# Turns of the probabilities placed after the odd step's second layer, earlier divisors, and reordered weight sums in a fused attention and feed-forward kernel

## The chip, the cores and the metric

The kernel runs on one core of a Trainium2 chip. The time is the device time of one execution in microseconds (us). The core has five engines with instruction queues of their own that run in order: TensorE (PE, matmuls; its weight loads are listed as PEld), VectorE (DVE), ScalarE (ACT), GpSimd (POOL) and SyncE (SP, which issues all DMAs here). They wait for each other through semaphores.

## What is computed

Attention with a window of 16 and summaries of blocks of 32, and a feed-forward layer on its output. Shapes: 4 batches, 8 heads, 768 positions, 64 numbers a head; d_model 512, d_ff 2048.

```python
k_sum = k.reshape(B, H, nb, block, D).max(axis=3)
v_sum = v.reshape(B, H, nb, block, D).mean(axis=3)
scores_l = scale * np.matmul(q, k.transpose(0, 1, 3, 2))      # kept where |i - j| < 16
scores_s = scale * np.einsum('bhsd,bhnd->bhsn', q, k_sum) + np.log(block)
a = softmax(concatenate([scores_l_m, scores_s]))              # sum + 1e-9 as divisor
attn = np.matmul(a, concatenate([v, v_sum], axis=2))
x = attn.transpose(0, 2, 1, 3).reshape(B * S, H * D)
h = x @ w_in
g = h * np.tanh(softplus(h))
return g @ w_out
```

## The kernel before

**Units, groups, steps.** The 3072 tokens are 12 chunks of 256; two chunks are a group, so there are 6 groups of 512 tokens. A unit is one chunk and one pair of heads: 48 units, numbered 0 to 47, 8 to a group. The feed-forward work of a group is 16 steps, one for each 128 columns of d_ff: 96 steps. Each number is kept as an upper and a lower part, and each product is three matmuls (upper by upper, upper by lower, lower by upper).

**A step** has a first layer (`ff_in`, L502, or `ff_in_pair`, L733), Mish on ACT (`ff_act`, L509), a split of the result into upper `ah` (L518) and lower `al` (L520), and a second layer (`ff_out`, L530, 12 matmuls) that is issued two steps later, so that it finds its split made. Groups 0 and 1 use the plain first layer of 12 matmuls. From step 32 on (groups 2 to 5) two steps are done together as a 2 by 2 block product with seven products instead of eight: `ff_in_pair`, 42 matmuls of 256 columns in four PSUM banks, whose results DVE (L743 to L751) and ACT (L739, L742) combine. It needs seven sums of blocks of the weights for every pair of steps, each in two parts, and seven sums of blocks of x.

**Weight sums.** For each of the eight pairs of steps p of a group the sums are made once, in two halves: `first_sums` (L700, L701, then a rounding on ACT, L691, and a subtraction, L692) and `second_sums` (L706, L707 and two more roundings). Both work in one area of SBUF and store their results with DMAs into a DRAM tile `kept[p]`; two blocks are stored as they are (`keep_blocks`). In steps 19 to 32 each step makes one half, pairs 0 to 6 in turn, and steps 35 and 36 make pair 7. `load_sums` (L718) brings the sums of a pair (7 x 2 parts x 128 KB, 1.83 MB) back into one of two buffers, two pairs ahead, in two DMAs: the first four blocks, then the other three. All DMAs are issued by SP in the order of the program, and a store whose sums are not yet made holds up what is behind it.

**Attention in the pairs.** Two units go through together, every four steps from step 29 on (`begins`: 19, 22, 25, 29, 33, ...). At the odd step i: the scores (`att_scores`, L346) and maxima with the mask added (DVE, L367), the exponents of the first unit on ACT (L378), those of the second inside the next pair. `norms` makes the divisors on DVE (L393, L394) and has POOL multiply the probabilities by them (L398): the first unit at step i, the second at step i + 1. At step i + 2, `turns` transposes both units on PE (L404) and ACT copies them out (L408). At step i + 4 `values` multiplies them by the values (L430), and `x_sum` makes the sums of blocks of x, which wait in a list (`waiting`) and are taken from it by the steps. `loads` issues the queries and keys of a unit two ahead (L304, L322, L323), has POOL copy its key maxima in (L309), and, for the first of a batch's chunks, loads keys (L235) for the maxima (DVE, L273) and values (L239) for the means (DVE, L294) through one buffer in turn.

**The order of a pair** of steps i, i + 1 is written out by hand. PE's queue: first layer, second layer of step i - 2, values and scores (every other pair), turns (in the pairs between), second layer of step i - 1. DVE's: the combining of the products, split of step i, divisors of the second unit, sums of blocks of x, weight sums, maxima, split of step i + 1, divisors of the first unit.

Of the kernel before, what the change touches and what calls it, by code (L numbers as in the profile page):

```python
# [9 lines left out]
F32 = mybir.dt.float32  # L10
# [10 lines left out]
P = 128  # L21
# [4 lines left out]
CH = 256  # L26
# [5 lines left out]
NFC = DFF // P  # L32
# [19 lines left out]
WP = 512  # L52
# [14 lines left out]
def fused_kernel(ctx: ExitStack, tc: tile.TileContext, q0, qk, kt, v0, vw, vs, w_in, w_out, out):  # L67
# [398 lines left out]
    def att_blocks(ps, c, hp, n):  # L466
        g, half = divmod(c, CG)
        if not raws:
            raws.append(stage_words("x_blocks").rearrange("p (b t) -> p b t", b=4))
        k = slice(hp % 2, hp % 2 + n)  # L470
        nc.scalar.copy(x_block(hp // 2, half)[:, k], ps[:, :n * CH].rearrange("p (k q) -> p k q", q=CH))
        made = {(0, 0): (2,), (1, 0): (4,), (0, 1): (6,), (1, 1): (5, 1, 3, 7)}[hp // 2, half]
        return [lambda m=m: x_sum(g, m, k) for m in made]
# [37 lines left out]

    def ff_split(g, fc):

        a = st[g, fc]
        ah = ff.tile([P, TG], F32R, tag="ah", name=f"ah{g}_{fc}")
        al = ff.tile([P, TG], F32R, tag="al", name=f"al{g}_{fc}")

        (nc.scalar.copy if g == 0 else nc.vector.tensor_copy)(ah, a)  # L518
        st[g, fc] = ah, al
        return lambda: nc.vector.tensor_sub(al, a, ah.bitcast(F32))  # L520
# [145 lines left out]
    dram = ctx.enter_context(tc.tile_pool(name="dram", bufs=1, space=bass.MemoryType.DRAM))  # L666
    kept = [dram.tile([P, 7, 2, CH], F32, name=f"w_sums_{p}") for p in range(NFC // 2)]
    whole_steps = WHOLE * NFC
# [12 lines left out]

    def keep(p, part, first, step, t):
        n = t.shape[1] // CH
        nc.sync.dma_start(kept[p][:, first:first + (n - 1) * step + 1:step, part, :], quarters(t).bitcast(F32))

    def keep_blocks(p):
        for part, t in enumerate(home(p)):
            keep(p, part, 0, 1, t[:, CH:3 * CH])

    def split_sums(p, first, step, whole, upper):  # L690
        nc.scalar.copy(upper.bitcast(F32R), whole)  # L691
        nc.vector.tensor_sub(whole.bitcast(F32R), whole, upper)  # L692
        keep(p, 0, first, step, upper)
        keep(p, 1, first, step, whole)

    def first_sums(p):

        hi, lo = home(p)
        w, t = area[:, :2 * WP], area[:, 2 * WP:3 * WP]
        nc.vector.tensor_add(w, hi.bitcast(F32), lo.bitcast(F32))  # L700
        nc.vector.tensor_add(quarters(t), quarters(w)[:, 0::2], quarters(w)[:, 1::2])  # L701
        split_sums(p, 3, 3, t, area[:, 3 * WP:])

    def second_sums(p):
        w, t = area[:, :2 * WP], area[:, 2 * WP:3 * WP]
        nc.vector.tensor_sub(t, w[:, :WP], w[:, WP:])  # L706
        nc.vector.tensor_add(w[:, WP:3 * CH], w[:, WP:3 * CH], w[:, CH:WP])  # L707
        split_sums(p, 4, 1, t, area[:, 3 * WP:])
        split_sums(p, 2, 1, w[:, WP:3 * CH], w[:, :CH])

    def buffer(pair):
        at = pair % 2 * BUFFER
        return grounds["w_early"][:, at:at + BUFFER].rearrange("p (m part f) -> p m part f", m=7, part=2)

    def load_sums(pair):
        if pair < (NG - WHOLE) * NFC // 2:
            for some in (slice(0, 4), slice(4, 7)):
                nc.sync.dma_start(buffer(pair)[:, some].bitcast(F32), kept[pair % (NFC // 2)][:, some])  # L718

    def ff_in_pair(g, fc, pair, between):  # L720
# [4 lines left out]
        def products(*found):  # L725
            ps = ps_w.tile([P, TG], F32, tag="w", name=f"ph{g}_{fc}_{len(banks)}")
            banks.append(ps)
            for half, m in enumerate(found):
                wh, wl = (w[:, (4, 3, 1, 2, 6, 7, 5).index(m), part, :] for part in range(2))
                xh, xl = x_piece(g, m)  # L730
                for a in range(2):
                    for n, (w_, x) in enumerate(((wh, xh), (wh, xl), (wl, xh))):
                        nc.tensor.matmul(turned(ps[:, half * CH:(half + 1) * CH]), w_[:, a * P:(a + 1) * P],  # L733
                                         turned(x[:, a, :]), start=(a == 0 and n == 0), stop=(a == 1 and n == 2))
# [70 lines left out]
    def scores(i):  # L805
# [5 lines left out]
        return some  # L811

    def weight_sums(i):
        p, second = divmod(i - done - 2 * (i > whole_steps), 2)
        if p < NFC // 2 and (i <= whole_steps or i > whole_steps + 2):
            if not second:
                keep_blocks(p)
            (second_sums if second else first_sums)(p)

    for i in range(done, whole_steps):  # L820
        ff_in(*steps[i])
        ff_act(*steps[i])
        values(i)
        for unit_ in scores(i):
            att_exponents(*unit_)
        ff_split(*steps[i])()
        norms(i)
        loads(i)
        for sums_ in waiting[:2]:
            waiting.pop(0)()  # L830
# [7 lines left out]
    for i in range(whole_steps, len(steps), 2):  # L838
        pair = (i - whole_steps) // 2
        ff_in_pair(*steps[i], pair, lambda: [att_exponents(*late_exponents.pop()) for _ in late_exponents[:]])  # L840
        ff_act(*steps[i])
        ff_act(*steps[i + 1])
        ff_split(*steps[i])()
        norms(i)
        while waiting:
# [7 lines left out]
        if some:  # L853
            att_exponents(*some[0])
            late_exponents.extend(some[1:])
        turns(i + 1)
        ff_split(*steps[i + 1])()
        norms(i + 1)
        loads(i + 1)
        for _ in waiting[:2]:  # L860
            waiting.pop(0)()
        ff_out(*steps[i - 1])
        weight_sums(i + 1)
    for i in range(2):
# [45 lines left out]
```

## Time and profile before

| | us |
|---|---|
| median of 3 runs | 680.04 |
| lowest and highest of them | 678.96, 682.68 |
| the profiled execution | 682.73 |
| span of its instructions | 681.0 |
| busy: PE, weight loads, DVE, ACT, POOL | 623.0, 535.1, 465.7, 309.8, 81.5 |
| mean granted clock of TensorE in it | 0.964 of full |

All rows below are of the profiled execution, in us from the start of its span. A matmul's duration is modelled, so a run of matmuls is read by its length as a whole; the waits and the start times are what counts.

### The profile page before, as it was taken

The page shows a single profiled execution, that of the slowest core. Times are in us where ns is not written, and L with a number is a line of the kernel's source. Part 1 is how long each engine was busy: PE and PEld are TensorE (multiplying, and loading weights), DVE is VectorE, ACT ScalarE, POOL GpSimd, SP SyncE. Part 2 cuts the span into 40 slices and gives each one's busy share as a digit, 9 for nine tenths or more (in the row PEclk, how much of TensorE's full clock was granted, in tenths as well). Part 3 has the DMA queues.
Part 4 walks back from the last instruction along what each step waited for, and adds up shares of the span by engine and source line. Part 5 has one row for each costly group of instructions (what it writes and reads, how often), then busy time and mean ns, then how long its engine had stood idle before and what let it go on. Part 6 is the DMA issues. An engine that isn't in the chain of part 4 may idle for free.

```text
span 681.0 us, 12911 instructions
## 1 busy us (share of the span) xinstructions
PE 623.0 (91%) x4848; PEld 535.1 (79%) x4848; DVE 465.7 (68%) x1158; ACT 309.8 (45%) x747; POOL 81.5 (12%) x119
## 2 busy tenths in 40 slices
PE   4799999999999977798988988889889899999997
PEld 3688777788887756687977887779778787998996
DVE  4799999964677688865648567657674474755443
ACT  4786769663555242643525335335263352122121
POOL 4431121110221010101001000010010000000000
PEclk9999999999998997888989999989899898999999
DMA  8787676623567689878547387585494454374421
GB/s 256 214 279 258 217 232 217 209 84 127 186 183 234 203 268 307 273 260 321 169 170 274 132 287 245 198 305 169 164 339 157 152 186 161 119 275 177 153 104 63
DMA packets 56366, 141.77 MB, mean 208 GB/s; under 512 B 8816, under 2 KB 28016, under 8 KB 52208
## 3 DMA queue, kind: packets, MB, share of 16 engines
q1 hardware_dynamic: 56304, 140.94, 61.4%
q8 instruction: 39, 0.64, 0.4%
q14 instruction: 23, 0.19, 0.1%
HBM read 117.83 MB, written 20.97 MB: 204 GB/s over the span
## 4 chain that ended last, share of the span: by engine, by line
PE 39%; DVE 14%; DMA 8%; ACT 4%; POOL 2%; issue 1%; SPq 1%; POOLq 0%; ACTq 0%; DVEq 0%
PE po L530 20%; PE ph L733 14%; DMA w_sums<-results 4%; DMA qk<-qk 3%; DVE al L520 2%; ACT pr L378 2%; POOL pr L398 1%; DVE pr L367 1%; PE x_ps L430 1%; PE pt_ps L404 1%; PE sc L346 1%; DVE ah L518 1%; DMA ks<-kt 1%; DMA vsum<-vs 1%; ACT h L509 1%
## 5 line engine op out<-in xcount | busy, mean ns | idle before, releaser
L530 PE MATMUL po<-w_early_out_hi,ah 128*128 128x512 f32 x240 | 100.5, 419 | 0.0
L733 PE MATMUL ph<-xh,w_early_in 128*128 128x256 f32 x512 | 98.7, 278 | 0.0
L530 PE MATMUL po<-w_early_out_hi,al 128*128 128x512 f32 x240 | 97.8, 408 | 0.9 <-DVE al L520 0.9
L530 PE MATMUL po<-w_early_out_lo,ah 128*128 128x512 f32 x240 | 97.8, 407 | 0.0
L398 POOL TENSOR_TENSOR pr<-pr,rs 128x480 f32<-128x480 f32 x48 | 59.6, 1243 | 292.8 <-DVE rs L394 253.8
L743 DVE TENSOR_TENSOR change<-h,ph 128x256 f32<-128x256 f32 x32 | 13.5, 421 | 102.6 <-ACT h L742 102.5
L733 PEld LDWEIGHTS ph<-xh,w_early_in 128*128 128x128 f32 x512 | 82.7, 189 | 0.0
L378 ACT ACTIVATE pr<-pr,nm 128x120 f32<-128x120 f32 x192 | 73.4, 386 | 12.2 <-DVE nm L367 11.9
L509 ACT ACTIVATE h<-h 128x512 f32<-128x512 f32 x64 | 36.9, 624 | 75.0 <-DVE h L750 75.0
L733 PE MATMUL ph<-xl,w_early_in 128*128 128x256 f32 x256 | 71.0, 277 | 0.0
L739 ACT COPY h<-ph 128x512 f32<-128x512 f32 x32 | 18.8, 587 | 101.6 <-PE ph L733 101.6
L404 PE MATMUL pt_ps<-ident,pr 128*120 128x128 f32 x192 | 32.4, 302 | 29.7 <-POOL pr L398 29.7
L530 PE MATMUL po<-w_late_out_hi,ah 128*128 128x512 f32 x144 | 59.2, 411 | 0.0
L530 PE MATMUL po<-w_late_out_hi,al 128*128 128x512 f32 x144 | 57.5, 399 | 0.0
L530 PE MATMUL po<-w_late_out_lo,ah 128*128 128x512 f32 x144 | 57.4, 399 | 0.0
L530 PEld LDWEIGHTS po<-w_early_out_hi,al 128*128 128x128 f32 x240 | 48.2, 201 | 10.8 <-DVE al L520 2.1
L530 PEld LDWEIGHTS po<-w_early_out_hi,ah 128*128 128x128 f32 x240 | 48.4, 202 | 10.2 <-issue 1.3
L530 PEld LDWEIGHTS po<-w_early_out_lo,ah 128*128 128x128 f32 x240 | 47.7, 199 | 10.4
L404 PEld LDWEIGHTS pt_ps<-ident,pr 128*120 128x120 f32 x192 | 23.2, 146 | 36.6 <-POOL pr L398 33.0
L502 PE MATMUL ph<-xh,w_early_in 128*128 128x512 f32 x160 | 52.0, 391 | 0.0
L520 DVE TENSOR_TENSOR al<-h,ah 128x512 fp32r<-128x512 f32 x64 | 48.4, 756 | 2.2
L733 PEld LDWEIGHTS ph<-xl,w_early_in 128*128 128x128 f32 x256 | 48.6, 190 | 0.0
(111 smaller groups left out, 1251.5 us busy)
## 6 DMA issues: line engine op xcount, KB each, us to landing
w_early_in<-w_sums SPq DMA_DIRECT2D x32, 1024.0 KB
w_early_in<-w_sums SPq DMA_DIRECT2D x32, 768.0 KB
qk<-qk SPq DMA_DIRECT2D x40, 496.0 KB
w<-w_in SPq DMA_DIRECT2D x16, 512.0 KB
w<-w_out SPq DMA_DIRECT2D x16, 512.0 KB
w_sums<-results SPq DMA_DIRECT2D x32, 256.0 KB
vw<-vw SPq DMA_DIRECT2D x40, 192.0 KB
ks<-kt SPq DMA_DIRECT2D x16, 384.0 KB
```

Of the source, the lines that this page charges most:

```text
L346: nc.tensor.matmul(ps[h][row, at0:at0 + KA], u["qk"][r, s, h * QT:(h + 1) * QT], u["qk"][r, s, P:], start=True, stop=True)
L367: nc.vector.tensor_tensor_reduce(out=pr[:, j, :], in0=ps[h][:, at + pair * KA:at + (pair + 1) * KA], in1=m, scale=-SCALE, scalar=-NEG, op0 ...
L378: nc.scalar.activation(pr[:, s, :], pr[:, s, :], AF.Exp, scale=-1.0, bias=nm[:, s:s + 1], accum_out=sm[:, s:s + 1])
L398: nc.gpsimd.tensor_mul(u["p"], u["p"], u["r"].unsqueeze(2).broadcast_to([P, NQ, KA]))
L404: nc.tensor.transpose(ps[:KA, s * P:(s + 1) * P], u["p"][:, s, :], ident)
L502: nc.tensor.matmul(turned(ph), w[:, cc * P:(cc + 1) * P], turned(x[:, cc, :]), start=(cc == 0 and n == 0), stop=(cc == NCC - 1 and n == 2))
L509: nc.scalar.activation(a, st[g, fc], AF.Mish)
L520: return lambda: nc.vector.tensor_sub(al, a, ah.bitcast(F32))
L530: nc.tensor.matmul(turned(po[g][t]), a[:, tok], turned(w), start=(fc == 0 and n == 0), stop=(fc == NFC - 1 and n == 2))
L733: nc.tensor.matmul(turned(ps[:, half * CH:(half + 1) * CH]), w_[:, a * P:(a + 1) * P], turned(x[:, a, :]), start=(a == 0 and n == 0), stop ...
L739: nc.scalar.copy(second, products(1, 3))
L743: nc.vector.tensor_sub(change, second[:, high], ps[:, low])
```

## The change

1. **Turns.** In a pair, `turns(i + 1)` is called after `ff_out(steps[i - 1])` instead of ahead of the split of step i + 1. Since the second layer is PE's and the split is DVE's, this moves the eight transposes of a turn behind 12 matmuls on PE, and their two ACT copies with them.
2. **Divisors.** In a pair, `norms(i)` stands ahead of `ff_split(steps[i])` instead of behind it.
3. **Weight sums.** The halves are made in the order of pairs 5, 0, 1, 2, 3, 4 in steps 19 to 30, none in steps 31 to 35, and pairs 6 and 7 in steps 36 to 39 (`order_of_sums`).
4. **Layout.** `kept[p]` holds the parts ahead of the blocks, and the blocks in an order in which two made together lie side by side, so that a store writes them as one run of 2 KB to a partition instead of two of 1 KB. `load_sums` brings the upper part and then the lower part, seven blocks each.
5. **Steps 19 to 31.** In a step without scores the upper part of the split is made by ACT instead of DVE, and only one waiting sum of x is taken, not two; in a step with scores the upper part is issued ahead of the exponents.
6. **x sums.** The last four of a group are made in the order 1, 5, 3, 7 instead of 5, 1, 3, 7.

```diff
-        made = {(0, 0): (2,), (1, 0): (4,), (0, 1): (6,), (1, 1): (5, 1, 3, 7)}[hp // 2, half]
+        made = {(0, 0): (2,), (1, 0): (4,), (0, 1): (6,), (1, 1): (1, 5, 3, 7)}[hp // 2, half]
...
-    def ff_split(g, fc):
+    def ff_split(g, fc, by_scalar=False):
...
-        (nc.scalar.copy if g == 0 else nc.vector.tensor_copy)(ah, a)
+        (nc.scalar.copy if g == 0 or by_scalar else nc.vector.tensor_copy)(ah, a)
...
-    kept = [dram.tile([P, 7, 2, CH], F32, name=f"w_sums_{p}") for p in range(NFC // 2)]
+    kept = [dram.tile([P, 2, 7, CH], F32, name=f"w_sums_{p}") for p in range(NFC // 2)]
...
-        nc.sync.dma_start(kept[p][:, first:first + (n - 1) * step + 1:step, part, :], quarters(t).bitcast(F32))
+        nc.sync.dma_start(kept[p][:, part, first:first + n, :], quarters(t).bitcast(F32))
...
-        split_sums(p, 3, 3, t, area[:, 3 * WP:])
+        split_sums(p, 3, t, area[:, 3 * WP:])
...
-        split_sums(p, 4, 1, t, area[:, 3 * WP:])
-        split_sums(p, 2, 1, w[:, WP:3 * CH], w[:, :CH])
+        split_sums(p, 5, t, area[:, 3 * WP:])
+        split_sums(p, 2, w[:, WP:3 * CH], w[:, :CH])
...
-            for some in (slice(0, 4), slice(4, 7)):
-                nc.sync.dma_start(buffer(pair)[:, some].bitcast(F32), kept[pair % (NFC // 2)][:, some])
+            for part in range(2):
+                nc.sync.dma_start(buffer(pair)[:, part].bitcast(F32), kept[pair % (NFC // 2)][:, part])
...
-                wh, wl = (w[:, (4, 3, 1, 2, 6, 7, 5).index(m), part, :] for part in range(2))
+                wh, wl = (w[:, part, (4, 3, 1, 2, 5, 6, 7).index(m), :] for part in range(2))
...
+    order_of_sums = {done + k: (p, k % 2) for k, p in enumerate((5, 5, 0, 0, 1, 1, 2, 2, 3, 3, 4, 4))}
+    order_of_sums.update({whole_steps + 4 + k: (6 + k // 2, k % 2) for k in range(4)})
+
     def weight_sums(i):
-        p, second = divmod(i - done - 2 * (i > whole_steps), 2)
-        if p < NFC // 2 and (i <= whole_steps or i > whole_steps + 2):
+        p, second = order_of_sums.get(i, (0, None))
+        if second is not None:
...
         values(i)
-        for unit_ in scores(i):
+        some = scores(i)
+        lower = ff_split(*steps[i], by_scalar=not some)
+        for unit_ in some:
             att_exponents(*unit_)
-        ff_split(*steps[i])()
+        lower()
         norms(i)
         loads(i)
-        for sums_ in waiting[:2]:
+        for _ in waiting[:2 if some else 1]:
             waiting.pop(0)()
         ff_out(*steps[i - 2])
         turns(i)
...
         ff_act(*steps[i])
         ff_act(*steps[i + 1])
+        norms(i)
         ff_split(*steps[i])()
-        norms(i)
         while waiting:
...
             att_exponents(*some[0])
             late_exponents.extend(some[1:])
-        turns(i + 1)
         ff_split(*steps[i + 1])()
         norms(i + 1)
         loads(i + 1)
         for _ in waiting[:2]:
             waiting.pop(0)()
         ff_out(*steps[i - 1])
+        turns(i + 1)
         weight_sums(i + 1)
```

## Rows read from the trace of the kernel before

**Rows 1.** Stretches: start:end, length, each engine's busy us (instructions), granted clock, DMA share, GB/s.

```profile
240.00:277.00 37.00, 28.53 (x182) 24.09 (x181) 28.89 (x59) 12.98 (x34) 2.50 (x4) 0.82 0.79 265
277.00:577.00 300.00, 272.86 (x2204) 240.29 (x2203) 192.47 (x535) 130.66 (x328) 30.15 (x42) 0.95 0.64 221
580.00:660.00 80.00, 80.00 (x522) 72.76 (x521) 46.03 (x97) 18.06 (x34) 0.00 (x0) 1.00 0.48 175
```

**Rows 2.** PE's waits, 277 to 577 us: line, what for, us in total, times, longest.

```profile
PE pt_ps L404 <- POOL pr L398: 25.9, 11, 4.0
PE sc L346 <- POOL qk L309: 1.2, 1, 1.2
```

**Rows 3.** Chain of waits, 335 to 365 us: start, us, engine, what, line, instructions.

```profile
342.22 0.44 DVE ah L518
342.68 0.69 DVE al L520
...
343.84 1.01 POOL pr L398
...
344.89 1.01 PE pt_ps L404 x4
345.90 3.97 PE po L530 x12
349.88 4.77 PE ph L733 x42
...
357.36 1.08 PE x_ps L430 x32
358.44 0.98 PE sc L346 x32
359.43 2.92 PE po L530 x12
```

**Rows 4.** Chain of waits, whole span: second layers behind turns (first, one between, last).

```profile
290.04 4.33 PE po L530 x12
...
428.36 2.72 PE po L530 x12
...
564.35 3.98 PE po L530 x12
```

**Rows 5.** Chain of waits, 396 to 432 us: loads for one unit's key maxima and means.

```profile
400.79 3.72 DMA ks<-kt
404.53 0.96 DVE km L273
405.51 6.49 DMA vsum<-vs
```

**Rows 6.** POOL in order of time: start, us, line, operation; in brackets idle time before.

```profile
315.96 1.49 POOL L398 TENSOR_TENSOR pr<-pr,rs 128x480 f32<-128x480 f32 x1
...
413.25 0.26 POOL L309 COPY qk<-km 128x96 f32<-128x96 f32 x1 [13.50 <-DMA qk<-qk]
...
439.42 0.26 POOL L309 COPY qk<-km 128x96 f32<-128x96 f32 x1 [11.77 <-DMA qk<-qk]
```

**Rows 7.** PE in order of time, 249 to 274 us: the instructions that waited.

```profile
253.85 1.11 PE L404 MATMUL pt_ps<-ident,pr 128*120 128x128 f32 x4 [3.29 <-POOL pr L398]
...
257.17 2.90 PE L733 MATMUL ph<-w_early_in 128*128 128x256 f32 x12 [2.21 <-DMA w_early_in<-w_sums]
...
272.31 0.64 PE L346 MATMUL sc<-qk 64*64 64x120 f32 x16 [2.97 <-POOL qk L309]
```

**Rows 8.** Chain of waits, whole span: the longest store of weight sums in it.

```profile
266.04 8.41 DMA w_sums<-results
```

**Rows 9.** Groups by line, whole span: busy us, mean ns, idle before and its releasers.

```profile
L692 DVE TENSOR_TENSOR results<-results 128x512 fp32r<-128x512 f32 (+1 forms) x24 | 13.7, 600 | 7.7 <-ACT results L691 7.7
...
L691 ACT CAST results<-results 128x512 fp32r<-128x512 f32 (+1 forms) x24 | 12.5, 546 | 59.7 <-DVE results L706 28.3 <-DVE results L701 18.2 <-issue 12.7
...
L700 DVE TENSOR_TENSOR results<-w_late_in 128x1024 f32<-128x1024 f32 x3 | 3.7, 1222 | 1.5 <-DMA w_sums<-results 0.8 <-DMA out<-results 0.7
```

More of the change, by code (lines that the diff above doesn't have):

```diff
@@ L680, in quarters, with keep, split_sums @@
         return t.rearrange("p (b f) -> p b f", f=CH)
-    def keep(p, part, first, step, t):
+    def keep(p, part, first, t):
         n = t.shape[1] // CH
-        nc.sync.dma_start(kept[p][:, first:first + (n - 1) * step + 1:step, part, :], quarters(t).bitcast(F32))
+        nc.sync.dma_start(kept[p][:, part, first:first + n, :], quarters(t).bitcast(F32))
     def keep_blocks(p):
         for part, t in enumerate(home(p)):
-            keep(p, part, 0, 1, t[:, CH:3 * CH])
-    def split_sums(p, first, step, whole, upper):
+            keep(p, part, 0, t[:, CH:3 * CH])
+    def split_sums(p, first, whole, upper):
         nc.scalar.copy(upper.bitcast(F32R), whole)
         nc.vector.tensor_sub(whole.bitcast(F32R), whole, upper)
-        keep(p, 0, first, step, upper)
-        keep(p, 1, first, step, whole)
+        keep(p, 0, first, upper)
+        keep(p, 1, first, whole)
     def first_sums(p):
@@ L707, in second_sums @@
         nc.vector.tensor_add(w[:, WP:3 * CH], w[:, WP:3 * CH], w[:, CH:WP])
-        split_sums(p, 4, 1, t, area[:, 3 * WP:])
-        split_sums(p, 2, 1, w[:, WP:3 * CH], w[:, :CH])
+        split_sums(p, 5, t, area[:, 3 * WP:])
+        split_sums(p, 2, w[:, WP:3 * CH], w[:, :CH])
     def buffer(pair):
         at = pair % 2 * BUFFER
-        return grounds["w_early"][:, at:at + BUFFER].rearrange("p (m part f) -> p m part f", m=7, part=2)
+        return grounds["w_early"][:, at:at + BUFFER].rearrange("p (part m f) -> p part m f", m=7, part=2)
     def load_sums(pair):
         if pair < (NG - WHOLE) * NFC // 2:
-            for some in (slice(0, 4), slice(4, 7)):
-                nc.sync.dma_start(buffer(pair)[:, some].bitcast(F32), kept[pair % (NFC // 2)][:, some])
+            for part in range(2):
+                nc.sync.dma_start(buffer(pair)[:, part].bitcast(F32), kept[pair % (NFC // 2)][:, part])
     def ff_in_pair(g, fc, pair, between):
```

## The prediction

> **What bounds the kernel now.** I read first the table of stretches [rows 1]. From 580 to 660 us, where no attention work is left, TensorE (PE) is busy all 80 of 80 us at the full clock (2.4 GHz): there the kernel runs at the speed of its matmuls, and nothing in the change touches that part. From 277 to 577 us PE is busy 272.86 of 300 us and its mean granted clock is 0.95. From 240 to 277 us it is worse: 28.53 of 37 us at 0.82, with VectorE (DVE) at 28.89. So what can be won lies in 337 us of the 681. The list of PE's waits [rows 2] then says what the gaps of the long stretch are: 25.9 us in eleven pieces, each PE standing at the transposes ("turns") of a second unit until GpSimd (POOL) has normalized its probabilities, and one gap of 1.2 us at the scores. Last I read the chain of waits over one such place [rows 3], from top to bottom: the two splits of the even step (ah 0.44, al 0.69), then the divisors, POOL's multiplication 1.01, the four transposes, then a second layer of 12 matmuls that takes 3.97 us where one at the full clock takes 2.72 [rows 4]. That is the second half of the loss: after such a wait the clock is at its lower level (1.2 GHz) for a while.
>
> **Part 1, turns behind the odd step's second layer.** Nothing is added or removed: 8 transposes and two ScalarE (ACT) copies change places with 12 matmuls of 2.72 us [rows 4]. Those 12 need splits made in the pair before, so they wait for nothing. No DMA moves. On ACT the two copies now stand right ahead of the next pair's first copy out of PSUM, but that one needs 12 matmuls first, so it hides them; without this cover they would cost about 2 x 0.55 us (priced as the ACT copy of a 128x512 tile in [rows 9]).
>
> **Part 2, divisors ahead of the even step's split.** The divisors leave behind them 0.44 + 0.69 us of DVE work, so POOL starts about 1.2 us sooner with its idle gaps. Together the turn gets 2.72 + 1.2 = 3.9 us of cover against waits of 25.9 / 11 = 2.35 us on average, 4.0 at the longest [rows 2]. All eleven waits could go. POOL's multiplication takes 1.01 us in [rows 3] and 1.49 us in one row of [rows 6]; 0.5 us more would still fit in 3.9 - 2.35 = 1.5 us of slack. The Trainium skill ("GPSIMD Engine Reference", section Specifications) says that POOL shares its SBUF interfaces with VectorE, with contention when a DVE instruction has two SBUF inputs. The split's subtraction is of this kind and would now run beside the multiplication, so that rule speaks against the move. If every multiplication took the long row's time and lay on the path, eleven turns would give back 11 x 0.48 = 5 us; by the slack, none. The row of 1.49 us shows only that the time varies, not why.
>
> **What the two parts can return.** The waits: 25.9 us. The slow second layers: the eleven after the turns lie at 4.33 (first) to 3.98 (last), except two of about 2.7, of which one row stands [rows 4]; nine times about 1.37 over 2.72 is 12.3 us. The waiting transposes too ran slow (1.01 us for four, [rows 3]); at 0.2 us each I put 2.3 us, an estimate. Sum: **40.5 us** at most.
>
> **What is late next.** (a) Units 36 to 39 need new key maxima and value means, and their loads form one serial chain through a single buffer: keys 3.72, maximum 0.96, values 6.49 [rows 5], and behind these the queries, whose POOL copy ends at 413.25 + 0.26 and 439.42 + 0.26 [rows 6]. At the first, PE's scores waited already (the 1.2 us of [rows 2]); at the second they ran just in time. The turns do not set this chain. If PE arrives sooner it stands at the scores instead, so the two turns in front of these give back their 2 x 2.35 = 4.7 us, and such a longer wait may cost one slow second layer, 1.5 us. Bounds: 0 if the loads come sooner with the shorter period, 8 if both waits slow the clock. I take 6.5, because the chain's DMAs last as long whatever PE does.
>
> (b) Sums 6 and 7 are moved from steps 31, 32, 35, 36 to steps 36 to 39. A first half has DVE's 1.22 plus an addition and a subtraction of about 0.7 and 0.6, with an ACT rounding of 0.55 between them; a second half two additions, two roundings and two subtractions [rows 9]: 3.4 and 2.7 us of DVE, the same wherever they stand. In steps 31 to 33 they stood in front of the scores' maxima. In steps 36 and 37 they share DVE with maxima, splits and a block sum. Such a pair takes PE 4.77 + 2.72 + 1.08 + 0.98 + 2.92 = 12.5 us [rows 3, 4]; DVE's mean share of the long stretch, 192.47 of 300, is 8.0 us of that, and 6.1 more, with three waits of about 0.7 for ACT's roundings, makes 16. So DVE falls about 4 us behind, ACT waits in its queue on DVE's sums (59.7 us of idle time before roundings in the whole run, [rows 9]) and the divisors of step 38 are late. SP also stands: the queries and weights of steps 38 and 39 are issued behind the sums' stores. I let one turn keep its loss (2.35 + 1.4 + 0.2, so 4) and one scores wait arise (about 4 with its slow layer): **8 us**, between 0 and 12.
>
> (c) The transition, 240 to 277 us [rows 7]: 3.29 at a turn, 2.21 at the first pair's weight sums, 2.97 at the scores, and matmuls at the lower clock behind each. Without sums in steps 31 to 35 the DVE stand behind a store that took 8.41 us [rows 8] goes, and the scores' queries come a little sooner: 2.97 and about 1.6 of slow clock, 4.6 us. Against this, the weight sums are now loaded as two whole parts, and the first product needs both, where before it needed the first 1.05 MB of 1.83: 0.79 MB more at the 265 GB/s of this stretch [rows 1] is 3.0 us at the first pair; later pairs have well over a step between load and use. The Trainium skill ("DMA: Bandwidth & Descriptors", Specifications) gives some 358 GB/s from HBM for a core; by it the piece would take an estimated 2.2 us and the sum would be 0.8 us better. This stretch moved less than that. With about 1.2 us from the lighter DVE queue, net gain **2.8 us**; bounds -3 (the loads alone) and +8 (every wait there but the loads).
>
> (d) Nine splits' copies go from DVE (0.44) to ACT (nearest row 0.55): -0.1 to +0.2 us on each chain, hidden by the two steps until their second layer. The order 1, 5 of the block sums, one sum a step, and weight sum 5 first take the same instructions; the longer runs of the stores can only be bounded by the store waits of [rows 8]: between -2 and +3, taken as 0.
>
> **Sum.** 40.5 - 6.5 - 8 + 2.8 = 28.8 us. The profiled execution lasted 682.73 us (span 681.0), which gives 653.9. The median of the plain runs is 680.04, 2.7 lower; the same gain gives **651 us**.
>
> **Rivals.** *Cover everywhere:* DVE absorbs (b) in its idle time, as the mean of [rows 1] (192 of 300 us) suggests, and only (a) returns something: 40.5 - 5 + 5 = 40, 640 us. *Half is given back:* the faster pairs need the same bytes in less time (221 GB/s over the long stretch, [rows 1], becomes about 250), queries land later and scores wait where turns did, in about five of eleven periods: 20 us of gain, 660 us; for it speak the 13.50 us that POOL stood for queries [rows 6], against it that the loads are issued two pairs ahead. *The change does not do what it says:* turns wait as long in their new place because POOL stands behind its copy for the queries, not behind the divisors: that needs queries 3.9 us later at every turn; 680. *Slower:* the sums of steps 36 to 39. Each second half waits until its area's first stores have landed. With 8.41 us [rows 8] at each of four halves, and ACT, SP and PE standing behind, with the turn now directly ahead of the first layer: 4 x 8.41 + 4 x 1.5 slow layers = 40 us lost there, and with (a) and (c) at their bad ends (8 and 3) 40.5 - 40 - 11 = -10: 690 us. It decides from stores that land over some 7 us after issue at every half; the one such wait stood behind 1.8 MB of loads.
>
> **How the numbers follow.** Forecast 651 (own range 645 to 657): 0.52. Cover everywhere, 634 to 645: 0.22. Half given back, 657 to 670: 0.17. No change: 0.04. Slower: 0.05. The range 636 to 664 leaves out about 0.2: the 0.09 of the last two, and the far ends of the two others. A measurement of this kernel can tell about 0.5% from no change; the first three are all well below 676.6, so faster 0.91, same 0.04, slower 0.05.
>
> **What would show it.** Right: in the list of PE's waits, "pt_ps from POOL pr" nearly gone, second layers behind scores and turns at 2.7, two periods near units 36 to 39 with waits at the scores. (b) right: a wait at the turn of step 39 or the scores of step 41. (c) right: a longer wait of the first product on the weight sums, none at the scores of step 33. Wrong: turns that still wait, scores waits in most periods, or a clock that stays at its lower level without a wait before it.

## The result and the profile after

The changed kernel takes 652.72 us (median; 649.94 to 653.69), the kernel before 681.36 beside it: a ratio of 0.957 (0.953 to 0.962). A repeat of the same kernel beside four others gave 651.57 us and 0.959 (0.957 to 0.962). The profiled execution lasted 653.35 us with a span of 651.6, against 682.73 and 681.0 before.

The stretches of the profiled execution, cut at the matching places (columns as in [rows 1]):

```profile
240.00:272.00 32.00, 25.85 (x179) 21.81 (x178) 24.38 (x59) 14.62 (x37) 2.93 (x4) 0.84 0.79 263
272.00:560.00 288.00, 275.78 (x2277) 245.43 (x2276) 204.61 (x541) 130.04 (x324) 32.56 (x42) 0.98 0.69 241
560.00:640.00 80.00, 80.00 (x523) 72.81 (x522) 44.02 (x95) 18.06 (x34) 0.00 (x0) 1.00 0.43 156
```

PE is idle 12 us of the long stretch where it was idle 27, the granted clock is 0.98 instead of 0.95, and the part without attention work is what it was. The list of PE's waits in that stretch, the answer to [rows 2]:

```profile
PE sc L346 <- POOL qk L309: 9.2, 3, 3.9
PE pt_ps L404 <- POOL pr L398: 3.1, 2, 1.9
```

Eleven waits at the turns became two, 25.9 us became 3.1; one wait at the scores became three, 1.2 us became 9.2. Where nothing waits, the chain of waits (335 to 372 us, answering [rows 3]) is PE alone:

```profile
340.03 0.87 PE pt_ps L404 x8
340.90 4.78 PE ph L733 x42
345.69 2.72 PE po L530 x12
348.40 1.08 PE x_ps L430 x32
349.48 0.98 PE sc L346 x32
350.46 2.92 PE po L530 x12
353.38 4.77 PE ph L733 x42
358.15 5.45 PE po L530 x24
363.60 0.87 PE pt_ps L404 x8
```

The turn now stands behind both second layers (x24) and runs through (x8 in 0.87 us, where it was cut in two by the wait). From turn to turn it is 23.57 us; before, the same pieces took 27.64 us (344.89 to 372.53), with a wait of some 2 us at the turn and a slow layer behind it.

Where the 29 us came from, by the starts of first layers in both traces (in order of time on PE; lengths in us):

| from the first layer of step | to | before | after | difference |
|---|---|---|---|---|
| start of the span | 32 | 257.2 | 254.1 | -3.1 |
| 32 | 36 | 37.0 | 28.6 | -8.4 |
| 36 | 42 | 40.6 | 47.0 | +6.4 |
| 42 | 50 | 54.9 | 47.2 | -7.7 |
| 50 | 58 | 53.7 | 56.1 | +2.4 |
| 58 | 76 | 124.8 | 105.5 | -19.3 |
| 76 | last second layer | 108.9 | 109.0 | +0.1 |

Two stretches got longer: 36 to 42, where the weight sums 6 and 7 now are, and 50 to 58, where units need new keys. (The first row can be chance alone: the kernel with only the turns moved has the instructions of the kernel before ahead of step 32 and starts that step's first layer at 252.3; over all profiles it starts at 249 to 257 us.) PE's waits in the first of them:

```profile
308.11 0.65 PE L404 MATMUL pt_ps<-ident,pr 128*120 128x128 f32 x4 [1.90 <-POOL pr L398]
...
323.37 1.08 PE L346 MATMUL sc<-qk 64*64 64x120 f32 x16 [3.61 <-POOL qk L309]
```

Behind the first, the 42 matmuls of the first layer took 1.7 us longer than the 4.77 of an undisturbed one, behind the second a second layer 2.4 us longer. Why the turn of step 39 waited shows on PE, ACT and DVE (in order of time): ACT's roundings of the second half of sum 6 stood in its queue in front of its first copy out of PSUM (L739), though the 12 matmuls that the copy needs had started at 295.39. The roundings themselves stood for DVE: what they round is made by L706, which came last in a row of DVE work that left gaps of 0.7 us at most from 289.53 on (maxima, splits, sums of x and of weights).

```profile
295.39 1.52 PE L733 MATMUL ph<-w_early_in 128*128 128x256 f32 x12
```

```profile
299.39 0.68 DVE L706 TENSOR_TENSOR results<-results 128x512 f32<-128x512 f32 x1
```

```profile
300.15 0.93 ACT L691 CAST results<-results 128x512 fp32r<-128x512 f32 x2 [3.52 <-issue]
300.98 0.58 ACT L739 COPY h<-ph 128x512 f32<-128x512 f32 x1
```

Why the scores of step 41 waited shows on SP: the queries (L304) are issued behind the stores of sum 7 (L684), which waited for the sums on DVE and their rounding on ACT, and behind 1.83 MB of weight sums (L718), and landed some 9.6 us later.

```profile
311.19 1.05 SPq L684 DMA_DIRECT2D w_sums<-results  x2
312.33 0.90 SPq L718 DMA_DIRECT2D w_early_in<-w_sums  x2
313.32 0.38 SPq L304 DMA_DIRECT2D qk<-qk  x1
```

In the stretch 50 to 58, POOL's copies of the key maxima and the multiplication between them, answering [rows 6]:

```profile
400.74 0.26 POOL L309 COPY qk<-km 128x96 f32<-128x96 f32 x1 [15.25 <-DMA qk<-qk]
...
416.48 0.26 POOL L309 COPY qk<-km 128x96 f32<-128x96 f32 x1 [10.14 <-DMA qk<-qk]
416.93 1.02 POOL L398 TENSOR_TENSOR pr<-pr,rs 128x480 f32<-128x480 f32 x1 [0.18 <-DVE vq L295]
...
429.19 0.26 POOL L309 COPY qk<-km 128x96 f32<-128x96 f32 x1 [11.23 <-DMA qk<-qk]
```

Before, the first of these copies ran at 413.25 and the last at 439.42 [rows 6]; 26.2 us lay between them, and now 28.5, though the pairs around them got shorter. What the queries of step 53 waited for shows in the chain of waits: SP issues the load of the values (L239) only when the key maximum has freed the buffer, and the queries (L304) stand behind that issue; the 1.83 MB of weight sums were issued 4 us ahead of them as well. At step 57 it is the same (keys 417.70, maximum 420.89, queries 422.32).

```profile
388.25 3.43 DMA ks<-kt
391.71 0.95 DVE km L273
...
393.12 7.46 DMA qk<-qk
```

And the transition, PE's waits from 248 to 270 us, answering [rows 7]:

```profile
252.13 1.11 PE L404 MATMUL pt_ps<-ident,pr 128*120 128x128 f32 x4 [3.48 <-POOL pr L398]
254.07 0.76 PE L733 MATMUL ph<-w_early_in 128*128 128x256 f32 x2 [0.83 <-DVE w_early_in L464]
256.24 2.50 PE L733 MATMUL ph<-w_early_in 128*128 128x256 f32 x10 [1.40 <-DMA w_early_in<-w_sums]
268.24 0.64 PE L346 MATMUL sc<-qk 64*64 64x120 f32 x16 [0.44 <-POOL qk L309]
```

The turn waits as before. The first products wait in two pieces (0.83, by this trace for DVE, and 1.40 for the weight sums) where they waited in one (2.21); in the repeat's profile both pieces are for the weight sums and longer (2.10 and 1.55). The scores' 2.97 are 0.44 (0.66 in the repeat).

### The profile page after: what moved, and what is told of

Same layout as the page of the kernel before. It is cut to its first block, busy times and chain, and to the rows that moved or that the text cites. A ratio compares the mean times of both kernels' runs of the same rounds, so it can differ in the third digit from the quotient of the medians.

```text
span 651.6 us, 12943 instructions
## 1 busy us (share of the span) xinstructions
PE 611.5 (94%) x4848; PEld 527.8 (81%) x4848; DVE 464.2 (71%) x1149; ACT 314.5 (48%) x756; POOL 85.3 (13%) x119
## 4 chain that ended last, share of the span: by engine, by line
PE 43%; DMA 6%; DVE 3%; ACT 1%; issue 1%; POOL 0%; SPq 0%; POOLq 0%; DVEq 0%
PE po L530 22%; PE ph L733 18%; DMA qk<-qk 4%; DMA vsum<-vs 1%; PE sc L346 1%; PE x_ps L430 1%; PE pt_ps L404 1%; DMA ks<-kt 1%; ACT pr L378 0%; DVE km L273 0%; DVE vq L294 0%; DVE al L520 0%; DVE pr L367 0%; DVE ah L518 0%; ACT h L509 0%
## 5 line engine op out<-in xcount | busy, mean ns | idle before, releaser
L530 PE MATMUL po<-w_early_out_hi,ah 128*128 128x512 f32 x240 | 96.6, 402 | 0.0
L530 PE MATMUL po<-w_early_out_hi,al 128*128 128x512 f32 x240 | 95.2, 397 | 0.2 <-DVE al L520 0.2
L530 PE MATMUL po<-w_early_out_lo,ah 128*128 128x512 f32 x240 | 95.2, 396 | 0.0
L530 PE MATMUL po<-w_late_out_hi,ah 128*128 128x512 f32 x144 | 57.1, 397 | 0.0
L530 PE MATMUL po<-w_late_out_hi,al 128*128 128x512 f32 x144 | 55.9, 388 | 0.0
L530 PEld LDWEIGHTS po<-w_early_out_hi,ah 128*128 128x128 f32 x240 | 46.4, 193 | 10.2 <-issue 1.7
L530 PEld LDWEIGHTS po<-w_early_out_hi,al 128*128 128x128 f32 x240 | 46.3, 193 | 9.1 <-DVE al L520 0.6
L520 DVE TENSOR_TENSOR al<-h,ah 128x512 fp32r<-128x512 f32 x64 | 51.0, 798 | 2.2
L739 ACT COPY h<-ph 128x512 f32<-128x512 f32 x32 | 18.7, 586 | 66.8 <-PE ph L733 60.3
L733 PE MATMUL ph<-w_late_in,w_early_in 128*128 128x256 f32 x320 | 47.1, 277 | 0.0
L309 POOL COPY qk<-km 128x96 f32<-128x96 f32 x40 | 19.6, 494 | 207.6 <-DMA qk<-qk 168.3
```

What stands on the lines that cost most here:

```text
L309: nc.gpsimd.tensor_copy(units[c, hp]["qk"][:, :, P + KW:], km.unsqueeze(1).broadcast_to([P, NQ, NB]))
L530: nc.tensor.matmul(turned(po[g][t]), a[:, tok], turned(w), start=(fc == 0 and n == 0), stop=(fc == NFC - 1 and n == 2))
L739: nc.scalar.copy(second, products(1, 3))
```

## The experiments

**One part alone: the turns.** The kernel before, with `turns(i + 1)` moved behind the second layer.

```diff
-        turns(i + 1)
         ff_split(*steps[i + 1])()
...
         ff_out(*steps[i - 1])
+        turns(i + 1)
```

> The kernel before with one edit: the turns of a pair stand behind the odd step's second layer; divisors, weight sums and layout as before. Theory (the 2.72 us of matmuls in front of the turn cover its wait): PE's waits at the turns in the pairs fall from 25.9 us in eleven to under 3 us, the slow second layers behind them go, and only the units with new keys give time back at the scores; 28 to 34 us of gain, 647 to 653 us. Rival 1 (the divisors are needed as well): the waits only fall by about half, 10 to 20 us of gain. Rival 2 (the wait moves with the turn, because what it waits for is itself set by PE's pace): under 5 us of gain.

Measured: 649.09 us, ratio 0.954 (0.948 to 0.960). PE's waits from 272 to 560 us:

```profile
PE sc L346 <- POOL qk L309: 5.6, 3, 2.7
PE pt_ps L404 <- POOL pr L398: 2.3, 2, 1.9
```

The move alone brings the whole gain of the change; neither rival holds. The turns' waits are gone as the theory said, and the scores wait at the two places with new keys (2.35 and 2.74 us) and for 0.55 us at step 37.

**One part alone: the divisors.** The kernel before, with `norms(i)` ahead of the even step's split.

```diff
+        norms(i)
         ff_split(*steps[i])()
-        norms(i)
```

> The kernel before with one edit: the divisors of the second unit stand ahead of the even step's split; turns, weight sums and layout as before. Theory: POOL starts about 1.1 us sooner at each turn, so the eleven waits fall from 25.9 us to about 13, and the slow second layers behind them become rarer; 12 to 22 us of gain, 659 to 669 us. Rival (POOL stands behind its copy for the queries, not behind the divisors): waits as before, under 3 us of gain.

Measured: 662.26 us, ratio 0.974 (0.968 to 0.979). PE's waits in the same stretch, and one of the usual turns:

```profile
PE pt_ps L404 <- POOL pr L398: 16.9, 11, 4.0
```

```profile
338.34 0.65 PE L404 MATMUL pt_ps<-ident,pr 128*120 128x128 f32 x4 [0.66 <-POOL pr L398]
```

Usual waits fell from 2.0 to 0.66 us, and behind those no slow layer is left; three long ones stay (4.00, 2.68 and 3.79 us), each with a slow layer. The gain is 18 us, more than the 9 us that the waits account for. The rival (POOL held by its copy for the queries) is out for the usual turns.

**The rest alone: sums, layout, splits.** The changed kernel with the two edits above taken back.

> The changed kernel with turns and divisors put back to their old places: what is left is the new order and places of the weight sums, the layout of the stored sums, the splits by ACT in steps 19 to 31 and the order of the sums of x. Theory: the stretch of 240 to 277 us gets some 3 us shorter, the turn at step 35 waits less, the one at step 39 more; 676 to 682 us. Rival (the sums in steps 36 to 39 cost several waits): 684 us or more. Rival (the spread sums bring a good part of the whole gain): under 670 us.

Measured: 680.37 us, ratio 0.999 (0.996 to 1.003). Nothing on balance, within the theory's range. From the turn of step 31 to the first layer of step 34 it is 25.4 us instead of 27.4, and the turn of step 35 waits 2.02 us instead of 3.97. The turn of step 39, which waited 2.73 us before, is the longest wait at a turn in these traces:

```profile
310.07 1.11 PE L404 MATMUL pt_ps<-ident,pr 128*120 128x128 f32 x4 [7.01 <-POOL pr L398]
```

**The divisors taken back.** The changed kernel with only `norms(i)` behind the split, measured twice.

> The changed kernel with one edit undone: the divisors of the second unit stand behind the even step's split again. Theory (the second layer in front of the turn already covers the usual wait of 2.0 to 2.3 us): only turns that still wait in the changed kernel, that of step 39 (1.9 us), wait 1.1 us longer; 652 to 656 us, against 652.7 for the whole change. Rival (both are needed): waits of about 1 us come back at most turns, 660 to 668 us.

> The changed kernel with the divisors of the second unit back behind the split, once more and in more rounds, on the same chip as the two others. Theory (the second layer in front of the turn covers the wait by itself): ratio to the kernel before within 0.004 of the changed kernel's 0.957 to 0.959. Rival (the divisors bring something on their own on top of the turns): 0.963 or more. Rival (they cost something, since the waits at the scores that they lead to are longer): 0.953 or less.

Measured: 649.84 us, ratio 0.954 (0.950 to 0.958), and 652.45 us, 0.959 (0.955 to 0.963), where the whole change had 0.957 and 0.959. So the divisors bring nothing that can be told once the turns are moved, and the first reading, a little below, does not come back. In the second profile one turn waits 4.1 us, that of step 39, 2.2 us more than in the changed kernel's first profile and 1.9 more than in its repeat (1.1 expected), and all others none; the waits at the scores are shorter in return (6.4 us in three, against 10.7 in three in the changed kernel's repeat).

**The changed kernel beside the next three.**

> The changed kernel itself, beside the next three on the same chip: 649 to 655 us.

Measured: 651.57 us, as told above.

**Sums 6 and 7 back in their old steps.**

```diff
-    order_of_sums.update({whole_steps + 4 + k: (6 + k // 2, k % 2) for k in range(4)})
+    order_of_sums.update({whole_steps + at_: (6 + k // 2, k % 2) for k, at_ in enumerate((-1, 0, 3, 4))})
```

> The changed kernel with sums 6 and 7 back in steps 31, 32, 35 and 36 (pair 5 still first). Theory (the sums in steps 36 to 39 make the turn of step 39 and the scores of step 41 wait, the latter through SP, which stands behind the stores of sum 7 before it issues the queries): in the changed kernel's profile these two waits are 1.9 and 3.6 us with 1.7 and 2.4 us of slow matmuls behind; here the wait at step 41 is under 1 us, while the wait at the scores of step 33 is back at 2 to 3 us, with slow matmuls, and the maxima of step 33 are late; net 2 to 6 us less than the changed kernel. Rival (what makes the scores of step 41 wait is the shorter period, not the sums): that wait stays at 3 us or more, and the time is the changed kernel's or some 3 us above.

Measured: 649.04 us, ratio 0.955 (0.952 to 0.958), 2.5 us below the repeat, though the two intervals overlap. The wait at the scores of step 41 is gone, as the theory said, so the sums and not the shorter period cause it. But the wait at step 33 is only 0.80 us, not 2 to 3, and others stand in its place: the turn of step 35 waits 3.55 us, that of step 39 2.48 and the scores of step 37 1.09. So the short wait at step 33 does not come from taking the sums out of steps 31 and 32. DVE's rows show why a half is dear there: it waits in DVE's queue for stores out of the area in which the sums are made.

```profile
285.97 1.23 DVE L700 TENSOR_TENSOR results<-w_late_in 128x1024 f32<-128x1024 f32 x1 [3.04 <-DMA out<-results]
...
297.77 0.69 DVE L706 TENSOR_TENSOR results<-results 128x512 f32<-128x512 f32 x1 [3.78 <-DMA w_sums<-results]
```

**Weight sums loaded by blocks again.** The changed kernel, new layout, with each load taking four or three blocks of both parts.

```diff
-            for part in range(2):
-                nc.sync.dma_start(buffer(pair)[:, part].bitcast(F32), kept[pair % (NFC // 2)][:, part])
+            for some in (slice(0, 4), slice(4, 7)):
+                nc.sync.dma_start(buffer(pair)[:, :, some].bitcast(F32), kept[pair % (NFC // 2)][:, :, some])
```

> The changed kernel with the weight sums loaded as four blocks of both parts and then three (as before the change), in the new layout. Theory (the first pair's products wait for all 1.83 MB): the wait inside the first pair's products (1.4 us in the changed kernel's profile) goes, no other place changes; 1 to 3 us less than the changed kernel, or no difference that can be told. Rival (two whole parts of 7 KB runs land sooner): the same or 1 to 3 us more.

Measured: 658.2 us, ratio 0.969 (0.966 to 0.971): 6.6 us more than the repeat, past what either side expected. The wait of the first products on the DMA went, as the theory said, though PE stood there 2.9 us for other releasers (2.14 of it put down to ACT's rounding L691); and the scores of steps 41, 53 and 57 waited 13.6 us, where the changed kernel had 9.2 and its repeat 10.7. In the new layout these loads are runs of 4 and 3 KB instead of 7, and there are more packets for the same bytes (lines of the two pages, changed kernel first):

```profile
DMA packets 50223, 141.78 MB, mean 218 GB/s; under 512 B 8816, under 2 KB 15728, under 8 KB 50160
```

```profile
DMA packets 58414, 141.77 MB, mean 215 GB/s; under 512 B 8816, under 2 KB 15728, under 8 KB 58352
```

The queries for step 41, which come behind such a load, took 8.97 us in the repeat and 10.07 here (chains of waits, repeat first):

```profile
311.85 8.97 DMA qk<-qk
```

```profile
316.39 10.07 DMA qk<-qk
```

In the changed kernel's first profile the same load took 9.59 us. The queries for steps 53 and 57 took 9.12 and 8.53 us here, against 7.75 and 7.26 in the repeat. That goes with the longer waits at the three scores. But from the first layer of step 32 to the end this profile is only 2.4 us longer than the repeat's (403.2 against 400.8; 397.6 in the first profile), and 4.3 us of the difference lie ahead of step 25, where neither kernel loads weight sums. So the traces bear out 2.4 to 5.6 us of the 6.6, and the rest stays open. With the old layout the runs were 8 and 6 KB, so this kernel is no picture of the kernel before. It points to the length of the runs but does not show it alone: the two loads are also 1.05 and 0.79 MB here instead of twice 0.92.

**Queries one step sooner.** The changed kernel, with the DMA of the second unit's queries issued in the even step, ahead of the stores and loads of weight sums on SP.

```diff
-        att_queries(c, hp)
+        if (c, hp) not in units:
+            att_queries(c, hp)
...
             put("keys", i + 2 * j, u + 2)
+            if j and i > whole_steps:
+                put("queries", i + 1, u + 2)
...
     def loads(i):
+        for unit_ in found("queries", i):
+            att_queries(*unit_)
```

> The changed kernel with the queries of a pair's second unit issued one step sooner (in the even step, ahead of the weight sums' stores and loads on SP); key maxima and POOL's copy stay where they are. Theory (the scores wait because SP issues the queries late and behind 1.8 MB of weight sums, not because the serial chain of key and value loads is too long): the waits at the scores of steps 41, 53 and 57 (3.6, 3.9 and 1.7 us in the changed kernel's profile) fall below 1 us each; 6 to 12 us less than the changed kernel. Rival (the serial chain through the one buffer sets them, as the prediction put it): step 41 improves, steps 53 and 57 keep 2 us or more; 2 to 6 us less. Rival (the queries only take the place of the weight sums in the queue): the first products of pairs wait for weight sums instead, no gain.

Measured: 644.42 us, ratio 0.948 (0.946 to 0.951), 7 us below the repeat. All three waits at the scores are gone, with the loads of keys and values as long as before (3.24 and 6.39 us in the chain of waits; 3.72 and 6.49 in [rows 5]). So the queries hung on that chain only by their place behind it in SP's queue: the rival is out, and the order of the queue is the cause. But a new wait stands at the turn of step 55 (4.92 us on PE), because POOL's copy of the next unit's key maxima, late for its queries and maxima, stands in front of the multiplication (POOL in order of time; lines from here on are shifted by up to four, L399 is the multiplication):

```profile
410.64 1.11 PE L405 MATMUL pt_ps<-ident,pr 128*120 128x128 f32 x4 [4.92 <-POOL pr L399]
```

```profile
408.93 0.71 POOL L309 COPY qk<-km 128x96 f32<-128x96 f32 x1 [9.85 <-DVE ah L519]
409.61 0.98 POOL L399 TENSOR_TENSOR pr<-pr,rs 128x480 f32<-128x480 f32 x1
```

**POOL's copy behind the multiplication.** As above, and the copy for a pair's first unit is issued one step later.

```diff
+            if i > whole_steps and u + 2 < len(todo):
+                put("queries" if j else "copies", i + 1, u + 2)
...
+        for unit_ in found("copies", i):
+            att_key_summary(*unit_)
```

> The kernel with early queries and one edit more: POOL copies the key maxima of a pair's first unit one step later, behind the multiplication of the second unit. With early queries alone one turn (step 55) waited 4.9 us and a slow first layer followed. Theory (there POOL stood at this copy, for the queries and maxima, in front of the multiplication): the wait at that turn falls below 1 us, the turn of step 39 keeps its 2.1 us, no new wait; 636 to 641 us, against 644.4 with early queries alone. Rival (the divisors or the exponents of that unit were late as well): it stays at 3 us or more, 643 to 646 us.

Measured: 639.52 us, ratio 0.941 (0.937 to 0.945). The wait at the turn of step 55 is 0.34 us; the one at step 39 keeps 2.10. Not all of the 4.92 us is won: the scores of step 57 now wait 1.6 us. The profile puts 1.0 of it down to a DMA of weight sums, which the scores do not read. They write PSUM banks of the pool that holds the products of the first layer, and DVE empties these late, because in its queue the key maximum (L273) stands in front, and DVE was idle there for the keys (PE and DVE):

```profile
413.62 0.39 PE L350 MATMUL sc<-qk 64*64 64x120 f32 x2 [1.02 <-DMA w_early_in<-w_sums]
```

```profile
411.17 0.95 DVE L273 TENSOR_REDUCE km<-ks 128x24 f32<-128x768 f32 x1 [3.08 <-DMA ks<-kt]
```

DVE's third combination (L749) ended at 413.36, 0.26 us ahead of these scores. By these rows what is left of the wait is the chain of loads again, through another queue.

**Sums 6 and 7 apart from the scores.** As above, with the halves in steps 36, 38, 39 and 42.

```diff
-    order_of_sums.update({whole_steps + 4 + k: (6 + k // 2, k % 2) for k in range(4)})
+    order_of_sums.update({whole_steps + at_: (6 + k // 2, k % 2) for k, at_ in enumerate((4, 6, 7, 10))})
```

> The kernel of late_copies and one edit more: sums 6 and 7 are made in steps 36, 38, 39 and 42, so that no half stands in a step with scores and its exponents. Theory (in the changed kernel the second half in step 37 holds up ACT's first copy of the next pair and with it the divisors of step 38): the wait at the turn of step 39 (1.9 to 2.1 us and 1.7 us of slow first layer) goes; 2 to 5 us less than late_copies. Rival (half 1 in step 36 alone makes step 38 late, or a half in step 39 or 42 makes another wait): the wait stays or moves, no gain.

Measured: 636.03 us, ratio 0.935 (0.931 to 0.939). From 272 us to the end PE waits 1.1 us in all:

```profile
PE pt_ps L408 <- POOL pr L402: 0.6, 1, 0.6
PE sc L350 <- DVE h L752: 0.5, 2, 0.3
```

What is left is the transition. ACT's rows there point at the cause of the turn's wait at step 31 (3.48 us here too): the rounding of step 29's half (L695 here) stands in front of the Mish of step 30 (L513), whose products had long been made. ACT stood 4.79 us before the rounding, for a sum on DVE that ended at 243.56.

```profile
243.64 0.62 ACT L695 CAST results<-results 128x512 fp32r<-128x512 f32 x1 [4.79 <-issue]
244.27 1.28 ACT L513 ACT_TABLE_LOAD   x1
245.57 0.60 ACT L513 ACTIVATE a<-ph 128x512 f32<-128x512 f32 x1
```

**No half in step 29.** As above, pair 4 in steps 30 and 31, and the first loads of weight sums ahead of the half of their step.

```diff
-    order_of_sums = {done + k: (p, k % 2) for k, p in enumerate((5, 5, 0, 0, 1, 1, 2, 2, 3, 3, 4, 4))}
+    order_of_sums = {done + k + (k > 9): (p, k % 2) for k, p in enumerate((5, 5, 0, 0, 1, 1, 2, 2, 3, 3, 4, 4))}
...
-        weight_sums(i)
-        if whole_steps - i in (3, 2):
-            load_sums(3 - (whole_steps - i))
+        if whole_steps - i in (3, 1):
+            load_sums(int(whole_steps - i == 1))
+        weight_sums(i)
```

> The kernel of spread_sums and one edit more: no half of a weight sum stands in step 29 (the last one with scores ahead of the pairs); pair 4 is made in steps 30 and 31, and the loads of weight sums for the first two pairs are issued in steps 29 and 31, ahead of that step's half. Theory (the turn of step 31 waits 3.3 to 3.5 us in every kernel so far because ACT's rounding of step 29's half stands in its queue in front of step 30's Mish): that wait falls below 1 us, the first pair's products wait less for the weight sums and run at the full clock; 5 to 9 us less than spread_sums, 627 to 631 us. Rival (that wait comes from DVE's own backlog of maxima, key maxima and sums of x): it stays above 2 us, and the time is within 2 us of 636. Rival (the halves in steps 30 and 31 hold up the first pair's combination instead): the wait moves to the scores of step 33, 634 us or more.

Measured: 628.52 us, ratio 0.925 (0.922 to 0.928), the fastest. PE's waits from 180 us to the end (the three largest):

```profile
PE ph L737 <- DMA w_early_in<-w_sums: 3.2, 2, 1.7
PE sc L350 <- POOL qk L309: 2.0, 2, 1.8
PE pt_ps L408 <- POOL pr L402: 0.5, 1, 0.5
```

The turn of step 31 waits no more, so DVE's maxima, key maxima and sums of x, which stayed, are not enough to hold it up. From that turn to the first layer of step 34 it is 19.0 us, against 23.7 in spread_sums. The edit takes the half's work on DVE out of the way together with ACT's rounding, and moves two loads, so it does not say how much each of them cost. By the ratios to the kernel before beside each, the gain is 6 us rather than the 7.5 between the medians. The first products still wait for the weight sums, 3.2 us instead of spread_sums' 1.9, and still run at the lower clock for 2.2 us (3.4 there): this half of the expectation did not hold.

## Why the prediction was right, point by point

The forecast was 651 us; 652.7 and, in the repeat, 651.6 were measured.

- **What bounds the kernel, and part 1.** Right: 25.9 of the 40.5 us stood in the first line of [rows 2]. The turns' waits went from 25.9 to 3.1 us, their slow layers from nine to one, and the move alone gives 31 us. Between steps 58 and 76 nothing else changes on PE: five turns gave back 19.3 us, 3.9 each, which is the 2.35 + 1.37 + 0.2 of the forecast. What the gain rests on was the cover of 2.72 us against 2.35 of mean wait.
- **Part 2.** The sum of 3.9 us of cover was right but more than was needed: each part alone takes off its share (31 and 18 us), and together they bring no more than the first. The prediction gave them one common price and so was not harmed; it did not say that the second part would be worth nothing on top.
- **The rule of the shared interface.** The Trainium skill ("GPSIMD Engine Reference", Specifications) holds in these traces. After the change the split's subtraction beside the multiplication takes about twice its 0.69 us [rows 3] (DVE in order of time):

```profile
307.25 1.35 DVE L520 TENSOR_TENSOR al<-h,ah 128x512 fp32r<-128x512 f32 x1
```

  The multiplications of the second units take 0.98 to 1.18 us from step 35 on, so the contention fell mostly on DVE and inside the slack, as reckoned.
- **(a), 6.5 us given back at units 36 to 39.** Right in size by the first profile: 3.87 + 1.16 + 1.69 us of waits and 1.3 of slow layer, less the 1.24 that stood there before, is 6.8. By the repeat it is 4.20 + 3.49 + 2.0 + 2.5 - 1.2 = 11, so the close match is partly luck. Half right in cause. The chain of loads does stand in front of the queries in the traces, as the prediction said. But it took this for fixed, and it hung only on order: the queries' place behind the chain in SP's queue, and the copy's place in POOL's. With both moved (late_copies), the loads of the chain are as long as they were and the waits there are 1.9 us in all, 0.3 at the turn and 1.6 at the scores.
- **(b), 8 us given back at steps 36 to 41.** Right in place and size: 1.9 + 1.7 at the turn of step 39 and 3.6 + 2.4 at the scores of step 41, 9.6 us. DVE was to fall about 4 us behind. Its first combination began 303.37 - 295.39 = 8.0 us after the first matmul of that pair, and 380.79 - 376.79 = 4.0 after that of step 50, which also follows scores: 4.0 behind. The way is the predicted one: ACT stood in its queue for DVE's sums, its copy behind the roundings, and SP issued the queries behind the sums' stores. The stretch from step 36 to 42, 47.0 us in the changed kernel and 45.2 in its repeat, is 40.3 us with the queries and the copy moved (late_copies) and 36.8 with the halves moved too (spread_sums). The sum behind the 4 us was not right, though: it gives a first half 3.4 us of DVE, where its own rows make 1.22 + 0.7 + 0.6 = 2.5, so it should have come out near 3; that it met the measured 4.0 is luck.
- **(c), 2.8 us won in the transition.** The sum held: from the turn of step 31 to the first layer of step 34 it is 23.6 us instead of 27.4, 3.8 won (25.1 and 2.2 in the repeat). Its terms did not all. The scores of step 33 gave 2.5 us of wait and 1.6 of slow layer, against 4.6; but with the sums back in steps 31 and 32 they wait only 0.80, so the reason given for it is not borne out, and the true one stays open. The two whole parts were to cost 3.0 us at the first pair. From the turn of step 31 to the end of that pair's products it is 15.2 us, and 16.5 in the repeat, against 14.9 before: 0.4 to 1.7, so this term was mis-sized by 1.3 us or more. The 1.2 us for a lighter DVE queue did not show at the turn: it waits 3.48 us, with step 29's half in front of it on DVE and ACT. Moving that half away removed the wait.
- **(d).** Not measured by itself, nor were the splits by ACT and the longer stores. Parts 3 to 6 together, without the first two, gave nothing (0.999), where the forecast's -8, +2.8 and 0 make -5.2; and the turns alone (0.954) cannot be told from the whole change.
- **The rivals.** *Cover everywhere* has the time of late_copies, 639.5 us against the 640 worked out for it, but by another order of two queues and with the wait at the turn of step 39 still there. *Half given back* is partly there: queries landed late, in three of eleven periods and not in five. *Slower* did not come: no half waited 8 us for a store; 1.16 us was the longest such wait of the moved halves in the changed kernel.

## What to carry to other kernels

A wait of one engine for another is removed by putting work that needs nothing new in front of it, for as long as the wait lasts; a second cure for the same wait is then worth little (nothing that could be told here), and should not be added to the sum. Before counting such a gain, go to the next place where the engine could stand if it came sooner, and read there which in-order queue (SP's issues, POOL's copies, ACT's roundings) puts work that nobody waits for yet ahead of what the engine needs: here three exchanges in such queues brought another 15 us, and one more the last 6 to 7.5. A transfer that is early enough itself still counts, if something urgent is issued behind it.

## What the runs showed of the hardware

- Loads of the same 1.83 MB in runs of 4 and 3 KB instead of 7 KB made 16% more packets in the whole kernel, and the queries issued behind such loads took 10.07, 9.12 and 8.53 us instead of 8.97, 7.75 and 7.26. The time was 1% longer (0.969 against 0.959), though every load is issued a pair or more ahead of its use; the traces show 2.4 to 5.6 us of that from step 32 on.
- A wait of some 2 us on PE is followed by a stretch at the lower clock at most turns of the kernel before (granted clock 0.50 from 345.6 to 347.0 us), which makes the second layer 1.4 us longer; behind two turns of 1.99 and 2.64 us it is not. A wait of 0.66 us is followed by none (the divisors alone): shortening most waits by two thirds gave back twice what it took off them.
- A two-input DVE subtraction took 1.35 us instead of 0.69 while POOL multiplied, and POOL's multiplication 1.17 instead of 0.99.
